# Selective attention with two key tiles per query tile, a bound checked on chip, and head-pair clusters between MLP subtiles

## The chip, the cores and the metric

The kernel runs on one core of a Trainium2 chip. The metric is device time in microseconds (us) of one execution; lower is better. The profile is one execution taken by the hardware profiler. Engines are named as there: PE is TensorE, PEld its weight loads, DVE is VectorE, ACT is ScalarE, POOL is GpSimd, SP is the queue that issues DMAs.

## The reference, cut to what matters

Causal attention over 8 batches, 8 heads, 576 tokens and 64 channels, with a penalty that grows with the summed positive part of `s` between key and query; then an MLP with exact GELU over the 4608 tokens.

```python
scores = scale * np.matmul(q, k.transpose(0, 1, 3, 2))
cum = np.cumsum(np.maximum(s, 0.0), axis=-1)
bias = -(cum[:, :, :, None] - cum[:, :, None, :])
scores = np.where(causal, -1000000000.0, scores + np.minimum(bias, 0.0))
attn = softmax(scores)            # with 1e-9 added to the sum
x = (attn @ v) as [4608, 512]
out = gelu_exact(x @ w_in) @ w_out    # 512 -> 2048 -> 512
```

`q`, `k` and `v` are normal draws times 0.1, `s` is a normal draw times 0.5, so `cum` rises by about 0.2 per token: a key 128 tokens back has a weight of about e^-25.

## The kernel before, in words

The penalty is a product: exp(cum of the key) goes into the values (`scale_v`, L158, with `wb`) and into the column of the denominator, and exp(-cum of the query) drops out in the quotient. So a head's attention is exp(scores), a mask on the diagonal tile, and two products with the same probabilities, one with the scaled values and one with `wb`.

Keys lie in five tiles of 128 (the last has 64). `UNITS` (L51) lists, per unit, the key tile, the first query, the number of queries and the place in PSUM; every key tile meets all later queries, 1600 columns per head. Two heads of a pair use the two halves of the PE array. `sc_item` (L232) is one unit of one pair: matmuls, one exp on ACT (L246), the mask on DVE (L254). `av_item` (L258) is one block of 256, 256 or 64 queries: numerator and denominator (L266), then Ln and Exp on ACT (L279, L280; the reciprocal) and the product into `xT` on DVE (L284).

The MLP works on nine chunks of 512 tokens. `l1_item` (L289): 8 matmuls of 512 columns and one GELU. `l2_item` (L305): a quarter of a 128-token subtile, 4 matmuls; after four quarters a copy to SBUF (L317) and a store.

Each engine runs its instructions in the order in which they are written (`manual_schedule`, L80). In chunk `c` (L373) the transposes of batch `c+1` (`tr_item`, L220, copies L228) lie between the L1 items; then `scale_v`, the table switch, the load and cast of batch `c+2`; then the 16 score items and 12 output items of batch `c+1` lie between 14 L2 quarters (`interleave`, L321). Chunks 7 and 8 have no attention beside them. Before the loop stand: the loads of batch 0, its casts and transposes, `scale_v(0)`, w_in, `load(1)`, the attention of batch 0 alone, `cast(1)`, w_out (L356 to L371). PSUM: `sc` (scores and L1) two buffers of two banks, `av` (outputs and transposes) two of one, `mlp` two of one.

Of the kernel before, what the change touches and what calls it, by code (L numbers as in the profile page):

```python
# [19 lines left out]
def kernel(  # L20
# [10 lines left out]
    nc = tc.nc  # L31
# [3 lines left out]
    MULT = mybir.AluOpType.mult  # L35

# [13 lines left out]

    UNITS = [  # L51
        [(0, 0, 512, 0)],
        [(1, 128, 448, 0), (0, 512, 64, 448)],
        [(2, 256, 320, 0), (3, 384, 192, 320)],
        [(4, 512, 64, 0)],
# [8 lines left out]
    LNC = [-28.0, 30.0, 60.0]  # L64
    ICH = [(0, 256), (256, 256), (512, 64)]
    PARTS, READY = [], []
    for c0, cn in ICH:
        parts = []
        for jt, i0, n, u, off in SEGS:
            lo, hi = max(i0, c0), min(i0 + n, c0 + cn)  # L70
            if lo < hi:
                parts.append((jt, lo - c0, hi - lo, off + lo - i0, u))
        parts.sort(key=lambda x: (-x[2], x[0]))
        PARTS.append(parts)
        READY.append(max(x[4] for x in parts))

    const = ctx.enter_context(tc.tile_pool(name="const", bufs=1))
    work = ctx.enter_context(tc.tile_pool(name="work", bufs=1))
    ps = ctx.enter_context(tc.tile_pool(name="ps", bufs=1, space=bass.MemoryType.PSUM))
    ctx.enter_context(tc.manual_schedule())  # L80
# [18 lines left out]
    nc.vector.tensor_copy(ident_bf, ident)  # L99
    lnb = const.tile([128, 3], fp32, name="lnb")  # L100
# [10 lines left out]
    qT = const.tile([128, NP, 640], bf16, name="qT")  # L111
    kT = const.tile([128, NP, 640], bf16, name="kT")
# [36 lines left out]

    def cast_pair(b, p):  # L150
        hs = slice(2 * p, 2 * p + 2)
        for i, n in enumerate(("q", "k")):
            t = raws[b, n]
            eng = nc.vector if i == 0 else nc.gpsimd
            eng.tensor_copy(qk_bf[:, i, 0 : ST - 1, hs], t[:, 0 : ST - 1, hs])
            eng.tensor_copy(qk_bf[:SL, i, ST - 1, hs], t[:SL, ST - 1, hs])
# [28 lines left out]

    def weights():
        s_pos = const.tile([64, S], fp32, name="s_pos")
        nc.vector.tensor_scalar_max(s_pos, s_sw, 0.0)
        sT = const.tile([128, ST, BH], fp32, name="sT")
        t_ps = ps.tile([128, ST, BH], fp32, tag="mlp", bufs=2, name="t_ps")  # L190
        for st in range(ST):
# [6 lines left out]
        c_ps = ps.tile([128, ST, BH], fp32, tag="mlp", bufs=2, name="c_ps")  # L198
        terms = [
            [(0, uptri_m1), (1, nones)],  # L200
            [(1, uptri_m1)],
            [(2, uptri)],
            [(2, ones), (3, uptri)],
            [(2, ones), (3, ones), (4, uptri)],
        ]
        for st in range(ST):
            n_st = 128 if st < ST - 1 else SL
            for i, (st2, m) in enumerate(terms[st]):
                n2 = 128 if st2 < ST - 1 else SL
                nc.tensor.matmul(  # L210
                    c_ps[:n_st, st, :], lhsT=m[:n2, :n_st], rhs=sT[:n2, st2, :],
                    start=(i == 0), stop=(i == len(terms[st]) - 1),
                )
# [5 lines left out]

    def tr_item(b, p, i):  # L220
        t_ps = ps.tile([128, 1024], bf16, tag="av", bufs=2, name="tr_ps")
        for st in range(ST):
            nc.tensor.transpose(  # L223
                t_ps[:, st * 128 : st * 128 + 128],
                qk_bf[:, i, st, 2 * p : 2 * p + 2, :].rearrange("p h d -> p (h d)"),
                ident_bf,
            )
        nc.vector.tensor_copy((qT, kT)[i][:, p, :S], t_ps[:, :S])  # L228
# [3 lines left out]
    def sc_item(b, p, u):  # L232
        if u == 0:
            P_of[b, p] = work.tile([128, 2, PW], bf16, tag="P", bufs=2, name="P")
        P = P_of[b, p]
        uw = UW[u]
        s_ps = ps.tile([128, 2, 512], fp32, tag="sc", bufs=2, name="sc_ps")
        for jt, i0, n, off in UNITS[u]:
            for e in range(2):
                nc.tensor.matmul(  # L240
                    s_ps[:, e, off : off + n],
                    lhsT=kT[e * 64 : e * 64 + 64, p, jt * 128 : jt * 128 + 128],
                    rhs=qT[e * 64 : e * 64 + 64, p, i0 : i0 + n],
                    start=True, stop=True,
                )
        nc.scalar.activation(  # L246
            P[:, :, UO[u] : UO[u] + uw], s_ps[:, :, :uw], func=AF.Exp, scale=scale
        )
        for jt, i0, n, off in UNITS[u]:
            if i0 != jt * 128:  # L250
                continue
            w = min(128, n)
            d = P[:, :, UO[u] + off : UO[u] + off + w]
            nc.vector.tensor_tensor(  # L254
                d, d, tri_bf[:, :w].unsqueeze(1).to_broadcast([128, 2, w]), op=MULT
            )

    def av_item(b, p, c):  # L258
        P = P_of[b, p]
        c0, cn = ICH[c]  # L260
        o_ps = ps.tile([128, 2, 256], fp32, tag="av", bufs=2, name="av")
        vb = vv[b % 2]
        for den in range(2):
            for n_part, (jt, lo, n, off, u) in enumerate(PARTS[c]):
                for e in range(2):
                    nc.tensor.matmul(  # L266
                        o_ps[e * 64 : e * 64 + 64, den, lo : lo + n],
                        lhsT=(
                            wb[:, jt, b * H + 2 * p + e : b * H + 2 * p + e + 1].to_broadcast([128, 64])
                            if den  # L270
                            else vb[:, jt, 2 * p + e, :]
                        ),
                        rhs=P[:, e, off : off + n],
                        start=(n_part == 0),
                        stop=n_part == len(PARTS[c]) - 1,
                        skip_group_check=True,
                    )
        ln = work.tile([128, 256], fp32, tag="ln", bufs=2, name="ln")
        nc.scalar.activation(ln[:, :cn], o_ps[:, 1, :cn], func=AF.Ln, scale=math.exp(-LNC[c]))  # L279
        nc.scalar.activation(  # L280
            ln[:, :cn], ln[:, :cn], func=AF.Exp, scale=-1.0, bias=lnb[:, c : c + 1]
        )
        t0 = b * S + c0
        nc.vector.tensor_tensor(xT[:, p, t0 : t0 + cn], o_ps[:, 0, :cn], ln[:, :cn], op=MULT)  # L284

# [3 lines left out]
    def l1_item(c, f2):  # L289
        if f2 == 0:  # L290
            gT_of[c] = work.tile([128, FT, NB], bf16, tag="gT", bufs=1, name="gT")
        h_ps = ps.tile([128, 2, NB], fp32, tag="sc", bufs=2, name="h_ps")
        for i in range(2):
            ft = f2 * 2 + i
            for ko in range(KO):
# [5 lines left out]
        nc.scalar.activation(gT_of[c][:, f2 * 2 : f2 * 2 + 2, :], h_ps, func=AF.Gelu)  # L301

    o_of = {}

    def l2_item(c, sub, part):  # L305
        if part == 0:
            o_of[c] = ps.tile([128, KO * 128], fp32, tag="mlp", bufs=2, name="o_ps")
        o_ps = o_of[c]
        gT = gT_of[c]
        for ft in range(part * 4, part * 4 + 4):  # L310
            nc.tensor.matmul(  # L311
                o_ps, lhsT=gT[:, ft, sub * 128 : (sub + 1) * 128], rhs=w_out_r[:, ft, :],
                start=(ft == 0), stop=(ft == FT - 1),
            )
        if part == 3:
            o_sb = work.tile([128, KO * 128], fp32, tag="osb", bufs=3, name="o_sb")
            nc.vector.tensor_copy(o_sb, o_ps)  # L317
            r0 = c * NB + sub * 128
            nc.sync.dma_start(out=out[r0 : r0 + 128, :], in_=o_sb)
# [18 lines left out]
    def attn_side(b, lag):  # L338

        items, due = [], []  # L340
        units = [(p, u) for p in range(NP) for u in range(NU)]
        for kk, (p, u) in enumerate(units):
            items.append(lambda p=p, u=u: sc_item(b, p, u))
            due += [(kk + lag, p, c) for c in range(len(ICH)) if READY[c] == u]
            while due and due[0][0] <= kk:
                _, p2, c2 = due.pop(0)
                items.append(lambda p=p2, c=c2: av_item(b, p, c))
        for _, p2, c2 in due:
            items.append(lambda p=p2, c=c2: av_item(b, p, c))
        return items  # L350

# [15 lines left out]
    for f in attn_side(0, 1):  # L367
        f()
    cast(1)
    for i in range(4):  # L370
        load_w(1, i)  # L371

    for c in range(NCH):  # L373
        nb = c + 1
        l1 = [lambda f2=f2: l1_item(c, f2) for f2 in range(FT // 2)]
        l2 = [lambda sub=sub, part=part: l2_item(c, sub, part) for sub in range(4) for part in range(4)]
        if nb < B:
            interleave(l1, tr_side(nb))
            scale_v(nb)
            exp_set()  # L380
            if nb + 1 < B:
                load(nb + 1)
                cast(nb + 1)
            interleave(l2[:14], attn_side(nb, 1), lead=1)
            for f in l2[14:]:
                f()
        else:
            for f in l1 + l2:
                f()
# [30 lines left out]
```

## Time and profile before

| | |
|---|---|
| median of 3 runs | 478.62 us (478.27 to 479.3) |
| the profiled execution | 474.67 us |
| its span, first to last instruction | 472.9 us |
| mean granted TensorE clock | 0.96 |
| busy | PE 391.3, ACT 263.7, DVE 177.1, POOL 44.2 us |

Read it by stages: a start until about 99 us, seven periods with attention beside the MLP, and two chunks of MLP alone. Busy time of PE counts each matmul from its start to its modelled end; what a matmul costs in a stream is the distance from one start to the next.

### The profile page before, as it was taken

To read this page: it belongs to the slowest core of one execution; us is meant where nothing else is said; L and a number is where in the kernel's file an instruction comes from. 1 tells how busy PE (TensorE), PEld (TensorE's weight loads), DVE (VectorE), ACT (ScalarE), POOL (GpSimd) and SP (SyncE) were. 2 spreads that over 40 slices of the span, in tenths; PEclk is the share of its full clock that TensorE was granted. 3 is DMA by queue.
4 is the path that set the end of the run, shared out by engine and by line. 5 is a ranking of instruction groups with operands and counts; after the bars stand their busy time and mean duration, and the time that the engine had idled before them with its cause. 6 is when DMAs were issued, how large, how long until landed. Compare 5 with 4: busy or idle time off the path is not lost.

```text
span 472.9 us, 8057 instructions
## 1 busy us (share of the span) xinstructions
PE 391.3 (83%) x3232; PEld 195.8 (41%) x3287; DVE 177.1 (37%) x425; ACT 263.7 (56%) x410; POOL 44.2 (9%) x49
## 2 busy tenths in 40 slices
PE   4310568579997999799979997999799989999996
PEld 4100334234453445344534453445344544444442
DVE  2314544264426442634263426342534244401101
ACT  1020575167846775677566756685658577751330
POOL 3100220040004000400040004000400000000000
PEclk9999967799999999999998999899989999999999
DMA  4448995960197019701870167118821000101101
GB/s 95 105 106 300 241 236 203 218 123 24 46 191 132 24 46 185 139 24 46 170 149 28 46 155 153 40 46 154 146 47 46 24 0 24 48 22 44 46 22 67
DMA packets 122757, 46.81 MB, mean 99 GB/s; under 512 B 113952, under 2 KB 113952, under 8 KB 122720
## 3 DMA queue, kind: packets, MB, share of 16 engines
q1 hardware_dynamic: 122720, 46.30, 42.3%
q8 instruction: 25, 0.41, 0.4%
q14 instruction: 12, 0.10, 0.1%
HBM read 36.85 MB, written 9.44 MB: 98 GB/s over the span
## 4 chain that ended last, share of the span: by engine, by line
PE 68%; DVE 10%; ACT 7%; SPq 7%; DMA 5%; issue 3%
PE h_ps L296 25%; PE o_ps L311 23%; PE av L266 13%; SPq L135 7%; ACT P L246 4%; PE sc_ps L240 4%; DVE vv_97 L163 3%; DVE vv_98 L163 3%; PE tr_ps L223 3%; DMA wf<-in_moe_w_in_dram 3%; DMA wf<-in_moe_w_out_dram 2%; DVE P L254 1%; ACT ln L279 1%; ACT ln L280 1%; DVE w_out_r L183 1%
## 5 line engine op out<-in xcount | busy, mean ns | idle before, releaser
L311 PE MATMUL o_ps<-w_out_r,gT 128*128 128x512 bf16 x538 | 140.3, 390 | 5.0 <-issue 4.4
L296 PE MATMUL h_ps<-xT,w_in_r 128*128 128x512 bf16 x559 | 135.2, 384 | 1.2 <-issue 0.3
L301 ACT ACTIVATE gT<-h_ps 128x1024 bf16<-128x1024 f32 x72 | 73.7, 1024 | 90.0 <-PE h_ps L296 90.0
L246 ACT ACTIVATE P<-sc_ps 128x1024 bf16<-128x1024 f32 (+1 forms) x128 | 102.8, 831 | 31.7 <-PE sc_ps L240 30.9
L296 PEld LDWEIGHTS <-w_in_r 128*128 128x128 bf16 x576 | 54.8, 99 | 58.0 <-issue 3.0
L311 PEld LDWEIGHTS <-gT 128*128 128x128 bf16 x576 | 48.4, 99 | 60.0 <-issue 13.2
L279 ACT ACTIVATE ln<-av 128x256 f32<-128x256 f32 (+1 forms) x96 | 31.4, 327 | 59.3 <-PE av L266 59.2
L254 DVE TENSOR_TENSOR P<-P,tri_bf 128x256 bf16<-128x256 bf16 (+1 forms) x160 | 42.5, 289 | 49.9 <-ACT P L246 49.8
L284 DVE TENSOR_TENSOR xT<-av,ln 128x256 bf16<-128x256 f32 (+1 forms) x96 | 34.3, 357 | 65.0 <-ACT ln L280 54.7
L266 PE MATMUL av<-P,vv_97 128*64 128x64 bf16 (+2 forms) x352 | 25.9, 256 | 34.2 <-DVE P L254 33.8
L240 PE MATMUL sc_ps<-qT,kT 64*128 64x64 bf16 (+4 forms) x384 | 43.6, 292 | 5.9 <-ACT P L246 5.9
L223 PE MATMUL tr_ps<-ident_bf,qk_bf 128*128 128x128 bf16 x320 | 30.6, 232 | 18.4 <-DVE qT L228 6.8
L280 ACT ACTIVATE ln<-ln,lnb 128x256 f32<-128x256 f32 (+1 forms) x96 | 43.6, 454 | 3.1
L317 DVE COPY o_sb<-o_ps 128x512 f32<-128x512 f32 x36 | 24.7, 686 | 53.0 <-PE o_ps L311 53.0
L266 PE MATMUL av<-P,wb 128*64 128x64 bf16 (+2 forms) x704 | 42.8, 240 | 0.0
L147 POOL CAST qk_bf<-raw_q 128x2048 bf16<-128x2048 f32 x7 | 13.3, 1896 | 272.9 <-DMA raw_k<-in_k_dram 126.3
L223 PEld LDWEIGHTS <-qk_bf 128*128 128x128 bf16 x320 | 24.2, 103 | 33.8 <-issue 7.6
L266 PEld LDWEIGHTS <-vv_97 128*64 128x64 bf16 x352 | 15.6, 120 | 49.0 <-issue 40.4
L228 DVE COPY kT<-tr_ps 128x576 bf16<-128x576 bf16 x32 | 14.6, 458 | 49.3 <-PE tr_ps L223 49.2
L240 PEld LDWEIGHTS <-kT 64*128 64x128 bf16 x384 | 15.0, 95 | 43.4 <-issue 37.5
L266 PE MATMUL av<-P,vv_98 128*64 128x64 bf16 (+2 forms) x352 | 23.5, 238 | 8.3 <-DVE P L254 7.8
L228 DVE COPY qT<-tr_ps 128x576 bf16<-128x576 bf16 x32 | 14.6, 458 | 41.7 <-PE tr_ps L223 41.7
(51 smaller groups left out, 159.7 us busy)
## 6 DMA issues: line engine op xcount, KB each, us to landing
out_dram<-o_sb SPq DMA_DIRECT2D x36, 256.0 KB, 2.0
raw_q<-in_q_dram SPq DMA_DIRECT2D x28, 256.0 KB, 5.0
raw_k<-in_k_dram SPq DMA_DIRECT2D x28, 256.0 KB, 5.4
raw_v<-in_v_dram SPq DMA_DIRECT2D x28, 256.0 KB, 4.5
wf<-in_moe_w_in_dram SPq DMA_DIRECT2D x4, 1024.0 KB, 5.3
wf<-in_moe_w_out_dram SPq DMA_DIRECT2D x4, 1024.0 KB, 7.7
raw_q<-in_q_dram SPq DMA_DIRECT2D x16, 64.0 KB, 2.2
raw_k<-in_k_dram SPq DMA_DIRECT2D x16, 64.0 KB, 2.2
```

The source lines that it names most:

```text
L135: nc.sync.dma_start(out=t[:n_st, st, h0 : h0 + hn, :], in_=bass.AP(tensor=src2.tensor, offset=src2.offset + (b * H + h0) * S * D + st * 12 ...
L223: nc.tensor.transpose(t_ps[:, st * 128 : st * 128 + 128], qk_bf[:, i, st, 2 * p : 2 * p + 2, :].rearrange("p h d -> p (h d)"), ident_bf,)
L240: nc.tensor.matmul(s_ps[:, e, off : off + n], lhsT=kT[e * 64 : e * 64 + 64, p, jt * 128 : jt * 128 + 128], rhs=qT[e * 64 : e * 64 + 64, p, ...
L246: nc.scalar.activation(P[:, :, UO[u] : UO[u] + uw], s_ps[:, :, :uw], func=AF.Exp, scale=scale)
L254: nc.vector.tensor_tensor(d, d, tri_bf[:, :w].unsqueeze(1).to_broadcast([128, 2, w]), op=MULT)
L266: nc.tensor.matmul(o_ps[e * 64 : e * 64 + 64, den, lo : lo + n], lhsT=(wb[:, jt, b * H + 2 * p + e : b * H + 2 * p + e + 1].to_broadcast([ ...
L279: nc.scalar.activation(ln[:, :cn], o_ps[:, 1, :cn], func=AF.Ln, scale=math.exp(-LNC[c]))
L280: nc.scalar.activation(ln[:, :cn], ln[:, :cn], func=AF.Exp, scale=-1.0, bias=lnb[:, c : c + 1])
L284: nc.vector.tensor_tensor(xT[:, p, t0 : t0 + cn], o_ps[:, 0, :cn], ln[:, :cn], op=MULT)
L296: nc.tensor.matmul(h_ps[:, i, :], lhsT=w_in_r[:, ko, ft * 128 : (ft + 1) * 128], rhs=xT[:, ko, c * NB : (c + 1) * NB], start=(ko == 0), st ...
L301: nc.scalar.activation(gT_of[c][:, f2 * 2 : f2 * 2 + 2, :], h_ps, func=AF.Gelu)
L311: nc.tensor.matmul(o_ps, lhsT=gT[:, ft, sub * 128 : (sub + 1) * 128], rhs=w_out_r[:, ft, :], start=(ft == 0), stop=(ft == FT - 1),)
```

## The change

Each query block meets two key tiles (256 columns per key tile, 192 and 64 at the end): 1024 columns per head, in two units. What is left out is bounded: `absmax` takes the largest |q| and |k| on DVE, `square_v` sums v squared on POOL, `cert_decay` and `cert_end` compare sums of the penalties and weights with limits, and one value `bad` decides at the end whether a general path, which computes everything anew with all keys, runs. With the inputs of the reference every comparison holds, worked out from them on paper (the largest: 67.5 against 78, 69.4 against 78, 0.256 against 0.375, 0.26 against 1), so the general path is skipped.

The order changes too. All scores of a pair and all outputs of the pair before it form one cluster, and whole L2 subtiles of 16 matmuls stand between clusters. L1 begins with two items without their last quarter. The last transposes stand behind L1. `load` and `cast` of batch `c+2` move behind the first L2 subtile and behind `square_v`. `av` gets three PSUM buffers, `mlp` one.

```diff
     UNITS = [
-        [(0, 0, 512, 0)],
-        [(1, 128, 448, 0), (0, 512, 64, 448)],
-        [(2, 256, 320, 0), (3, 384, 192, 320)],
-        [(4, 512, 64, 0)],
+        [(0, 0, 256, 0), (1, 128, 256, 256)],
+        [(2, 256, 256, 0), (3, 384, 192, 256), (4, 512, 64, 448)],
     ]
...
+    def absmax(b, p):
+        nc.vector.tensor_reduce(
+            amx[:, b * NP + p], qkT[:, :, p, :S], axis=AX, op=ALU.max, apply_absolute_value=True
+        )
+    def square_v(b):
+        t = raws[b, "v"]
+        for st in range(ST):
+            n_st = 128 if st < ST - 1 else SL
+            sq = work.tile([128, H, D], fp32, tag="sq", bufs=2, name="sq")
+            nc.gpsimd.tensor_tensor(sq[:n_st], t[:n_st, st], t[:n_st, st], op=MULT)
+            nc.gpsimd.tensor_tensor(sumv[:n_st], sumv[:n_st], sq[:n_st], op=ALU.add)
...
+    def cert_decay():
+        t_ps = ps.tile([1, ST + 1, BH], fp32, tag="av", bufs=3, name="ct_ps")
+        for st in range(ST):
+            n_st = 128 if st < ST - 1 else SL
+            nc.tensor.matmul(t_ps[:, st, :], lhsT=ones[:n_st, 0:1], rhs=sT[:n_st, st, :], start=True, stop=True)
...
+        nc.vector.tensor_copy(T, t_ps)
+        nc.vector.tensor_copy(W, w_ps)
...
+    def cert_end():
+        g = const.tile([128, 3], fp32, name="cg")
+        for i in range(2):
+            nc.vector.tensor_reduce(g[:, i : i + 1], amx[:, :, i], axis=AX, op=ALU.max)
+        nc.vector.tensor_reduce(
+            g[:, 2:3], sumv.rearrange("p h d -> p (h d)"), axis=AX, op=ALU.max
+        )
+        g_ps = ps.tile([3, 128], fp32, tag="av", bufs=3, name="cg_ps")
+        nc.tensor.transpose(g_ps, g, ident)
+        g3 = const.tile([3, 1], fp32, name="cg3")
+        nc.vector.tensor_reduce(g3, g_ps, axis=AX, op=ALU.max)
+        h_ps = ps.tile([1, 3], fp32, tag="av", bufs=3, name="ch_ps")
+        nc.tensor.transpose(h_ps, g3, ident[:3, :3])
...
+    def sc_item(b, p):
+        P_of[b, p] = P = work.tile([128, 2, PW], bf16, tag="P", bufs=2, name="P")
+        for u in range(NU):
+            s_ps = ps.tile([128, 2, 512], fp32, tag="sc", bufs=2, name="sc_ps")
...
+            nc.scalar.activation(
+                P[:, :, UO[u] : UO[u] + UW[u]], s_ps[:, :, : UW[u]], func=AF.Exp, scale=scale
+            )
+            d = P[:, :, UO[u] : UO[u] + 512].rearrange("p e (g c) -> p e g c", c=256)[:, :, :, 0:128]
+            nc.vector.tensor_tensor(
+                d, d, tri_bf.unsqueeze(1).unsqueeze(1).to_broadcast([128, 2, 2, 128]), op=MULT
+            )
+            if u == 1:
...
+    def av_item(b, p):
...
+        for c, (c0, cn) in enumerate(ICH):
+            o_ps = ps.tile([128, 2, 256], fp32, tag="av", bufs=3, name="av")
...
+            todo.append(o_ps)
+        for c, (c0, cn) in enumerate(ICH):
...
-    def l2_item(c, sub, part):
-        if part == 0:
-            o_of[c] = ps.tile([128, KO * 128], fp32, tag="mlp", bufs=2, name="o_ps")
+    def l2_item(c, sub):
         gT = gT_of[c]
-        for ft in range(part * 4, part * 4 + 4):
+        o_ps = ps.tile([128, KO * 128], fp32, tag="mlp", bufs=1, name="o_ps")
+        for ft in range(FT):
...
-    for f in attn_side(0, 1):
-        f()
+    for p in range(NP):
+        sc_item(0, p)
+        if p > 0:
+            av_item(0, p - 1)
+    av_item(0, NP - 1)
+    for p in range(NP):
+        absmax(0, p)
+    square_v(0)
     cast(1)
     for i in range(4):
         load_w(1, i)
+    cert_decay()
     for c in range(NCH):
         nb = c + 1
+        l1_item(c, 0, 0, KO - 1)
+        l1_item(c, 1, 0, KO - 1)
+        l1_item(c, 0, KO - 1)
+        l1_item(c, 1, KO - 1)
+        l1 = [lambda f2=f2: l1_item(c, f2) for f2 in range(2, FT // 2)]
         if nb < B:
-            interleave(l1, tr_side(nb))
+            tr = tr_side(nb)
+            interleave(l1, tr[:4])
+            for f in tr[4:]:
+                f()
             scale_v(nb)
             exp_set()
-            if nb + 1 < B:
-                load(nb + 1)
-                cast(nb + 1)
-            interleave(l2[:14], attn_side(nb, 1), lead=1)
-            for f in l2[14:]:
+            for p in range(NP):
+                sc_item(nb, p)
+                if p > 0:
+                    av_item(nb, p - 1)
+                l2_item(c, p)
+                absmax(nb, p)
+                if p == 0:
+                    square_v(nb)
+                    if nb + 1 < B:
+                        load(nb + 1)
+                        cast(nb + 1)
+            av_item(nb, NP - 1)
+        else:
+            for f in l1:
                 f()
-        else:
-            for f in l1 + l2:
-                f()
+            for sub in range(4):
+                l2_item(c, sub)
+            if c == B - 1:
+                cert_end()
+    fast.close()
+    rv = nc.values_load(bad[0:1, 0:1], min_val=0, max_val=1)
+    with tc.If(rv > 0):
...
```

## Rows read from the trace of the kernel before

**Rows 1.** The page: the chain that ended last, shares of the span by engine.
```profile
PE 68%; DVE 10%; ACT 7%; SPq 7%; DMA 5%; issue 3%
```

**Rows 2.** Windows by stage; columns in the first line.
```profile
core 0: us, PE busy (x) PEld busy (x) DVE busy (x) ACT busy (x) POOL busy (x), PEclk, DMA share, GB/s
130.45:178.30 47.85, 43.97 (x385) 21.75 (x392) 20.21 (x50) 31.93 (x51) 5.30 (x4) 0.96 0.49 97
...
369.56:414.36 44.80, 42.75 (x385) 21.37 (x392) 18.18 (x50) 31.86 (x51) 0.00 (x0) 1.00 0.07 25
...
152.00:153.50 1.50, 1.50 (x10) 0.69 (x10) 0.53 (x3) 0.60 (x2) 0.00 (x0) 0.50 0.81 116
153.50:155.40 1.90, 1.90 (x15) 0.84 (x15) 0.65 (x2) 0.57 (x2) 0.00 (x0) 0.56 0.02 4
```

**Rows 3.** Timeline of PE in L1: start, length, engine, line, count.
```profile
131.53 0.44 PE L223 MATMUL tr_ps<-ident_bf,qk_bf 128*128 128x128 bf16 x5
...
131.81 1.89 PE L296 MATMUL h_ps<-xT,w_in_r 128*128 128x512 bf16 x8
...
133.53 0.44 PE L223 MATMUL tr_ps<-ident_bf,qk_bf 128*128 128x128 bf16 x5
```

**Rows 4.** Timeline of PE among scores, outputs and L2 quarters.
```profile
107.05 0.57 PE L266 MATMUL av<-P,vv_98 128*64 128x256 bf16 x8
...
107.94 1.04 PE L311 MATMUL o_ps<-w_out_r,gT 128*128 128x512 bf16 x4
108.91 0.39 PE L240 MATMUL sc_ps<-qT,kT 64*128 64x512 bf16 x2
...
110.64 0.61 PE L240 MATMUL sc_ps<-qT,kT 64*128 64x448 bf16 x8
111.18 1.04 PE L311 MATMUL o_ps<-w_out_r,gT 128*128 128x512 bf16 x4
...
122.17 0.35 PE L266 MATMUL av<-P,vv_98 128*64 128x64 bf16 x10
...
122.61 1.04 PE L311 MATMUL o_ps<-w_out_r,gT 128*128 128x512 bf16 x4
```

**Rows 5.** Timeline where L1 gives way to attention; idle time and releaser in brackets.
```profile
144.07 1.90 POOL L147 CAST qk_bf<-raw_q 128x2048 bf16<-128x2048 f32 x1 [41.27 <-DMA raw_k<-in_k_dram]
...
146.42 5.30 DVE L163 TENSOR_TENSOR vv_97<-raw_v,wb 128x512 bf16<-128x512 f32 x5
...
151.98 0.53 PE L266 MATMUL av<-P,vv_97 128*64 128x256 bf16 x4 [2.40 <-DVE P L254]
```

**Rows 6.** The same DVE instructions in the last period with attention.
```profile
385.53 3.08 DVE L163 TENSOR_TENSOR vv_98<-raw_v,wb 128x512 bf16<-128x512 f32 x5
```

**Rows 7.** Groups by line: count | busy us, mean ns | idle before, releaser.
```profile
L246 ACT ACTIVATE P<-sc_ps 128x1024 bf16<-128x1024 f32 x96 | 94.3, 1019 | 26.0 <-PE sc_ps L240 25.2
...
L279 ACT ACTIVATE ln<-av 128x256 f32<-128x256 f32 (+1 forms) x96 | 31.4, 327 | 59.3 <-PE av L266 59.2
...
L280 ACT ACTIVATE ln<-ln,lnb 128x256 f32<-128x256 f32 (+1 forms) x96 | 43.6, 454 | 3.1
...
L317 DVE COPY o_sb<-o_ps 128x512 f32<-128x512 f32 x36 | 24.7, 686 | 53.0 <-PE o_ps L311 53.0
...
L155 POOL CAST qk_bf<-raw_k 128x512 bf16<-128x512 f32 x4 | 2.5, 615 | 18.0 <-DMA raw_k<-in_k_dram 18.0
```

**Rows 8.** Timeline at the end of the start: last w_out cast, PE, first score.
```profile
86.05 1.23 DVE L183 CAST w_out_r<-wf 128x2048 bf16<-128x2048 f32 x1 [4.02 <-DMA wf<-in_moe_w_out_dram]
...
87.70 0.69 PE L223 MATMUL tr_ps<-ident_bf,qk_bf 128*128 128x128 bf16 x5 [6.81 <-DVE qT L228]
...
99.37 0.39 PE L240 MATMUL sc_ps<-qT,kT 64*128 64x512 bf16 x2
```

**Rows 9.** The end: last copy (timeline); SP's waits: us, times, longest.
```profile
469.18 0.69 DVE L317 COPY o_sb<-o_ps 128x512 f32<-128x512 f32 x1 [2.76 <-PE o_ps L311]
...
SPq L415 <- PEq L415: 0.6, 2, 0.4
```

## Prediction before the run

> **What bounds the kernel now.** I read the page first, then the windows by stage, then PE's timeline inside a period. The chain of waits runs through PE for 68% of the span [rows 1], so the sum is one of PE's time, and other engines count where PE waits for them. Three kinds of stage follow the start [rows 2]: six periods of L1, transposes, attention and L2 (47.85 us in the one shown), a last such period without a load (44.80), and from 414.4 two chunks of MLP alone. A bare chunk is 128 matmuls of 512 columns. Eight of them take 133.53 - 131.81 = 1.72 us [rows 3], so a chunk takes 27.5, and attention costs a period about 20 us of PE. That is what the change cuts.
>
> Inside the period PE is dense but for one hole: the first output matmuls wait 2.40 us for the mask on DVE, which stands behind `scale_v` [rows 5], and after it the granted clock is 0.50, the lower of the two levels, 1.2 GHz, for 1.5 us and on average 0.56 for the next 1.9 [rows 2]: that costs 0.75 + 0.84 = 1.6 us more. In the last period the same five products take 3.08 us instead of 5.30 [rows 5, 6], POOL has no cast beside them, the clock stays at 1.00, and the period is 3.05 us shorter. So a POOL cast beside DVE's two-input products costs 3 us a period.
>
> **L1 with transposes.** A group of five transposes costs 131.81 - 131.53 = 0.28 us. The head (two items of six matmuls, then two of two) makes 14 matmuls before the first GELU can start, at 3.0 us; the GELU has the shape of the exp, which takes 1.02 [rows 7]; the third item needs its PSUM buffer, so it starts at 4.3 instead of 3.45. This is a new stall of 0.85 in all nine chunks. It buys the cover for the last output block: its Ln, Exp and product may end 2.6 us later than L1 begins. Then 6 x 1.72 + 3 x 0.28 = 11.15, and five transpose groups at the end, 1.7 us with three buffers. L1 ends at 17.15. The last GELU hides behind these transposes.
>
> **A cluster.** Scores: two units of 512 columns take 111.18 - 110.64 = 0.54 [rows 4]; before, four units. Outputs: the 256-query block took 107.94 - 107.05 = 0.89 for 1792 columns on a half of the array, 0.50 ns each, the last block 122.61 - 122.17 = 0.44 for 640, 0.69 ns each. After, 28 matmuls of 2048 columns in all: 1.02 by the one, 1.41 by the other; I take 1.2, since the wide blocks hold most columns. An L2 quarter takes 108.91 - 107.94 = 0.97, that is 0.86 and about 0.11 for the change of shape; a whole subtile 3.45 + 0.11 = 3.56. A pair costs 0.54 + 1.2 + 3.56 = 5.3.
>
> Do the others keep up? ACT per pair: two exps 2.04, and (31.4 + 43.6) / 32 = 2.34 for Ln and Exp [rows 7], 4.4 of 5.3. DVE: masks and products of 1728 elements 2.1 (by `scale_v`'s 0.62 for 512 [rows 6]), the copy 0.69 [rows 7], and the new `absmax` over 1152 elements. No such reduce is in the trace; by `scale_v`'s 3.08 for five times 512 [rows 6] it takes 1.4, by the copy's 0.69 for 512 [rows 7] 1.55, below that if bf16 runs faster; I take 1.4. Sum 4.2 of 5.3. The order also fits: output of pair p-1 comes a whole subtile after its exp, so a mask has 4 us to arrive. The first outputs come at 17.15 + 0.54 + 3.56 + 0.54 = 21.8, `scale_v` (from 17.8, 3.08) and two masks end at about 21.9. The hole of 2.40 us is covered by the subtile, as long as POOL is quiet.
>
> Attention is then 4 x 5.3 + 0.3 = 21.5, the period 38.65; with 0.3 for a mask that meets a cast I take **39.0**, against 47.85. Bounds: outputs 1.02 to 1.41 give 38.0 to 39.9.
>
> **The load and POOL.** `load` and `cast` go behind the first L2 subtile's store, 22 us into the period instead of at its start. The casts started 13.6 us into the period shown [rows 5], when the data had landed; now at about 35, with some 5 us of work, ending 1.5 us into the next L1. The first transposes come at 7.8, so 6 us of cover stay; each us beyond that would be PE's. On SP the stores of three subtiles queue behind 15 load issues; nobody waits, as the three output buffers last a period. SP's issue of v now also waits for `square_v` of the batch before, done 20 us earlier.
>
> `square_v` adds ten POOL instructions of 512 elements with two inputs per batch. The nearest row is the cast of 512 elements, one input, 0.615 [rows 7]; two inputs should lie between 0.6 and 1.25, and I take 1.2. The Trainium skill (GPSIMD Engine Reference, section on elementwise cycle accounting) gives 4497 ns for 2048 elements of such an add, an estimate of 1.12 for 512; by that the sum stays as it is. They run after the casts and after v has landed (half of what q and k took, 6.8 us later, at 42), so from 3 to 15 us into L1, where DVE only copies from PSUM. `scale_v` follows at 17.8. So the contention of before should vanish here, and by the same margin of 2.8 us it could come back (rivals).
>
> **The two bare chunks.** With one `mlp` buffer and nothing between subtiles, PE's next matmul waits for the copy, 0.69 [rows 7], and two hand-overs: 0.7 to 1.2, I take 0.95, three times in each chunk; behind it the rest of L2 is queued on PE and the GELUs of the next chunk on ACT. A chunk is 27.5 + 0.85 + 2.85 = 31.2. `cert_end` puts two transposes in front of L1 of the last chunk: PE waits for the copy (0.95), three reduces (about 0.9) and a further small reduce between them, 3.0 us with latencies (2 to 4.5), and then runs at the lower clock as after the 2.40 us hole, 1.6 more. Sum 31.2 + 3.0 + 1.6 + 31.2 = **67.0**, against 55.0.
>
> **The start.** Before, PE stood until 87.70 for DVE copies behind the last w_out cast, and the first score of batch 1 came 11.7 us later, at 99.37 [rows 8]. After, that cast moves: four `absmax` (5.6) are put in front of it, `square_v(0)` meets `scale_v(0)` and the w_in casts (0 to 5, I take 3), the attention of batch 0 is shorter (a pair by 0.54 for scores and, at 0.50 to 0.69 ns for 1152 columns, 0.6 to 0.8 for outputs, twice that at the lower clock; four pairs 5 to 10, I take 7), and `load(2)` no longer takes bandwidth (1). About 0.6 later: PE goes on at 88.3. `cert_decay` adds some 20 tiny DVE instructions behind it, about 3 us, covered by L1. With three `av` buffers PE has done five L1 items by then instead of three, so three are left: 5.2 + 0.85 for transposes, 1.7 for the last groups, 1.6 at the lower clock: scores start at 97.7 (92 to 102). I credit almost nothing here.
>
> **The tail.** From the last copy's start at 469.18 [rows 9] to the end of the span are 3.7 us, 3.9 with the hand-over before it; they stay. The register load, the branch and their barriers have no row; the nearest are SP's waits for other engines at the end, 0.6 together [rows 9], and that last chain itself, 3.7, done up to three times, 11. I take 5, nearer the low end, as only one value is read. The Trainium skill (Runtime: NRT & Kernel Launch, instruction fetch mechanics) says that a taken branch out of the fetched pages stalls for a fetch; no row shows one, and by that rule the 5 would be nearer 7.
>
> **The sum.** 97.7 + 21.5 (batch 1) + 6 x 39.0 + 67.0 + 3.9 + 5 = 429.1 of span, against 472.9. Around the span lie 474.67 - 472.9 = 1.8: 430.9. The median of the runs shown is 478.62, 0.83% over the profiled execution, so **434.5 us**.
>
> **The rivals.**
> (a) POOL meets `scale_v` and stops the next period: the squares run to 42 + 10X, that is 3 + 10X into L1. At X = 1.2 they end before 17.8. From X = 1.6 on they hold `scale_v` and the first masks, and PE waits 10X - 17 us in every period, plus 1.6 at the lower clock. Rows 5 and 6 show the mechanism; against it stands the 0.615 of rows 7. X = 1.6 to 2.1 gives 439 to 475. The page SBUF — State Buffer of the Trainium skill (Who interferes with whom) states that a GpSimd instruction and a two-input DVE instruction exclude each other for a whole instruction; 5.30 against 3.08 agrees.
> (b) Slower: the same place, X above 2.2. Then 7 x (10X - 15.4) is more than the 44 gained: 2.5 gives 502. It needs an instruction 3.6 times as long as the cast of as many elements.
> (c) DVE becomes the bound of the clusters: if `absmax` takes over 2.5 us, each further us costs 28. At 3.0, 449.
> (d) The bound fails and the general path runs: several milliseconds. The inputs speak against it.
> (e) Better: outputs at 0.50 ns (5 us), the start without contention (5) and a tail of 1 (4) give 420.
>
> **How the numbers follow.** Forecast (425 to 444) 0.55, (a) 0.14, (b) 0.06, (c) 0.07, (d) 0.01, (e) 0.13; the remaining 0.04 is a mixture that ends near the old time. The range takes in (e)'s end, (c) and most of (a): 419 to 460. Changes within 0.2% can't be told from none in this kernel. Slower by more than that: (b), (d) and half the mixture, 0.08; same 0.02; faster 0.90.
>
> **What would show it.** A window between two first L1 matmuls of 39 us with the clock at 1.00; `scale_v` at 3.1 us; squares at 1.2 each, ended before it; no idle time of PE before `av`; PE idle 0.95 before `o_ps` in the last chunks, released by DVE's copy; a gap of 3 us before the last L1. It would be wrong if PE waits in `av` for DVE while POOL is busy, if ACT has no idle time between exps, or if the pair takes over 5.6 with PE dense.

## The result and the profile after

The changed kernel takes 417.73 us (median of 4 runs, 416.19 to 418.4) against 478.44 for the kernel before in 4 runs: a ratio of 0.873, interval 0.870 to 0.877. The forecast was 434.5; the time lies 1.3 us below the low end of its range. The profiled execution took 417.87 us with a span of 416.0.

The chain of waits still runs through PE, now for three quarters of the span (before: [rows 1]):

```profile
PE 75%; SPq 8%; DMA 7%; DVE 4%; ACT 3%; issue 2%; ACTq 0%; DVEq 0%
```

Windows by stage, with the columns of [rows 2]: two of the six periods, then the two bare chunks.

```profile
116.24:153.95 37.71, 37.03 (x321) 20.03 (x322) 21.90 (x46) 26.60 (x43) 15.50 (x14) 1.00 0.59 120
153.95:191.67 37.72, 37.04 (x322) 20.02 (x322) 21.55 (x46) 26.61 (x43) 16.88 (x15) 1.00 0.61 125
...
342.52:372.00 29.48, 26.45 (x122) 11.65 (x121) 3.98 (x7) 11.01 (x14) 0.00 (x0) 1.00 0.10 36
372.00:416.00 44.00, 32.42 (x139) 13.69 (x137) 9.08 (x31) 8.08 (x8) 0.00 (x0) 0.91 0.09 32
```

A period fell from 47.85 to 37.71 us, and in it PE is busy for 37.03 us at full clock: 0.68 us is left, the stall in the head of L1. Of these windows the clock dips only in the last, behind the check's last comparison.

The timeline of POOL and DVE where L1 gives way to attention, the place of [rows 5]: first and last square, `scale_v`, the first masks.

```profile
156.50 1.03 POOL L173 TENSOR_TENSOR sq<-raw_v 128x512 f32<-128x512 f32 x1
157.61 1.27 POOL L174 TENSOR_TENSOR sumv<-sumv,sq 128x512 f32<-128x512 f32 x1
...
166.97 1.26 POOL L174 TENSOR_TENSOR sumv<-sumv,sq 64x512 f32<-64x512 f32 x1
...
171.70 3.08 DVE L189 TENSOR_TENSOR vv_101<-raw_v,wb 128x512 bf16<-128x512 f32 x5
174.70 0.75 DVE L357 TENSOR_TENSOR P<-P,tri_bf 128x512 bf16<-128x512 bf16 x2
```

The squares end 3.5 us ahead of `scale_v`, which takes the 3.08 us that it took before without a cast beside it [rows 6]. PE's waits say the same from the other side (us in total, times, longest):

```profile
PE av L375 <- DVE P L357: 23.7, 1, 23.7
PE tr_ps L332 <- DVE cT L268: 6.2, 1, 6.2
PE h_ps L413 <- ACT gT L419: 6.2, 9, 0.7
...
PE o_ps L425 <- DVE o_sb L430: 4.7, 6, 0.8
...
PE cg_ps L302 <- DVE cg L298: 1.6, 1, 1.6
```

PE waits for a mask once in the whole execution, in the start. The hole of 2.40 us in each period is gone.

The outputs of a pair on PE, with the next matmul behind them, and the last copy:

```profile
341.44 0.35 PE L375 MATMUL av<-P,vv_101 128*64 128x256 bf16 x4
341.63 0.33 PE L375 MATMUL av<-P,wb 128*64 128x256 bf16 x4
341.79 0.39 PE L375 MATMUL av<-P,vv_101 128*64 128x256 bf16 x6
342.01 0.39 PE L375 MATMUL av<-P,wb 128*64 128x256 bf16 x6
342.23 0.23 PE L375 MATMUL av<-P,vv_101 128*64 128x64 bf16 x4
342.29 0.23 PE L375 MATMUL av<-P,wb 128*64 128x64 bf16 x4
342.46 2.76 PE L413 MATMUL h_ps<-xT,w_in_r 128*128 128x512 bf16 x12
...
409.48 0.69 DVE L430 COPY o_sb<-o_ps 128x512 f32<-128x512 f32 x1 [3.70 <-PE o_ps L425]
```

The 28 output matmuls take 342.46 - 341.44 = 1.02 us. The last copy starts 6.5 us ahead of the end of the span; before it was 3.7 [rows 9].

### The profile page after: what moved, and what is told of

It is laid out like the page before. It is cut to its first block, busy times and chain, and to the rows that moved or that the text cites. A ratio compares the mean times of both kernels' runs of the same rounds, so it can differ in the third digit from the quotient of the medians.

```text
span 416.0 us, 7091 instructions
## 1 busy us (share of the span) xinstructions
PE 348.8 (84%) x2745; PEld 187.6 (45%) x2745; DVE 207.1 (50%) x441; ACT 221.3 (53%) x346; POOL 140.3 (34%) x130
## 4 chain that ended last, share of the span: by engine, by line
PE 75%; SPq 8%; DMA 7%; DVE 4%; ACT 3%; issue 2%; ACTq 0%; DVEq 0%
PE o_ps L425 31%; PE h_ps L413 28%; SPq L146 8%; PE av L375 8%; PE tr_ps L332 4%; PE sc_ps L347 4%; DMA wf<-in_moe_w_in_dram 3%; DMA wf<-in_moe_w_out_dram 3%; ACT gT L419 2%; DVE o_sb L430 1%; DVE w_out_r L209 1%; ACT P L353 1%; DVE w_in_r L203 1%; ACT ln L391 0%; ACT ln L392 0%
## 5 line engine op out<-in xcount | busy, mean ns | idle before, releaser
L425 PE MATMUL o_ps<-w_out_r,gT 128*128 128x512 bf16 x576 | 130.5, 379 | 4.7 <-DVE o_sb L430 4.7
L353 ACT ACTIVATE P<-sc_ps 128x1024 bf16<-128x1024 f32 x64 | 61.9, 1021 | 40.9 <-PE sc_ps L347 40.9
L337 DVE COPY qkT<-tr_ps 128x576 bf16<-128x576 bf16 x64 | 26.6, 453 | 85.2 <-PE tr_ps L332 85.0
L174 POOL TENSOR_TENSOR sumv<-sumv,sq 128x512 f32<-128x512 f32 (+1 forms) x40 | 52.1, 1302 | 3.1
L173 POOL TENSOR_TENSOR sq<-raw_v 128x512 f32<-128x512 f32 (+1 forms) x40 | 47.0, 1174 | 9.3 <-DMA raw_v<-in_v_dram 9.3
L163 DVE TENSOR_REDUCE amx<-qkT 128x2 f32<-128x1152 bf16 x32 | 42.7, 1341 | 0.0
L396 DVE TENSOR_TENSOR xT<-av,ln 128x256 bf16<-128x256 f32 (+1 forms) x96 | 33.7, 357 | 17.6 <-ACT ln L392 15.5
L375 PE MATMUL av<-P,vv_100 128*64 128x128 bf16 (+2 forms) x224 | 17.2, 248 | 27.1 <-DVE P L357 23.7
L375 PE MATMUL av<-P,wb 128*64 128x128 bf16 (+2 forms) x448 | 28.8, 237 | 0.0
L357 DVE TENSOR_TENSOR P<-P,tri_bf 128x512 bf16<-128x512 bf16 x64 | 27.4, 451 | 2.0 <-ACT P L353 1.7
L158 POOL CAST qk_bf<-raw_k 128x2048 bf16<-128x2048 f32 x7 | 13.3, 1894 | 27.8 <-DMA raw_k<-in_k_dram 15.6
```

The source lines that it names most:

```text
L163: nc.vector.tensor_reduce(amx[:, b * NP + p], qkT[:, :, p, :S], axis=AX, op=ALU.max, apply_absolute_value=True)
L173: nc.gpsimd.tensor_tensor(sq[:n_st], t[:n_st, st], t[:n_st, st], op=MULT)
L174: nc.gpsimd.tensor_tensor(sumv[:n_st], sumv[:n_st], sq[:n_st], op=ALU.add)
L353: nc.scalar.activation(P[:, :, UO[u] : UO[u] + UW[u]], s_ps[:, :, : UW[u]], func=AF.Exp, scale=scale)
L375: nc.tensor.matmul(o_ps[e * 64 : e * 64 + 64, den, lo : lo + n], lhsT=(wb[:, jt, b * H + 2 * p + e : b * H + 2 * p + e + 1].to_broadcast([ ...
L425: nc.tensor.matmul(o_ps, lhsT=gT[:, ft, sub * 128 : (sub + 1) * 128], rhs=w_out_r[:, ft, :], start=(ft == 0), stop=(ft == FT - 1),)
```

## The experiments

Each of the nine was timed beside the kernel before on the same chip; its medians there were 476.6 to 478.3 us. A difference between the medians of two experiments, or between one of them and 417.73, is therefore good to about 2 us; where less than that matters, the traces are compared. In every expectation, a "theory" is the prediction's sum with the terms that the trace after shows.

### Tiles alone, order alone

`e1_tiles_only`: the kernel before with one edit.

```diff
     UNITS = [
-        [(0, 0, 512, 0)],
-        [(1, 128, 448, 0), (0, 512, 64, 448)],
-        [(2, 256, 320, 0), (3, 384, 192, 320)],
-        [(4, 512, 64, 0)],
+        [(0, 0, 256, 0), (1, 128, 256, 256)],
+        [(2, 256, 256, 0), (3, 384, 192, 256), (4, 512, 64, 448)],
     ]
```

> The kernel before with the two-tile UNITS alone (1024 columns per head in two units), its order, its buffers and no bound computed: it leaves out the check and the general path. Theory (PE time of the dropped columns pays what it costs, the hole stays): a pair saves 0.54 us of scores and 0.6 to 0.8 of outputs, so a period goes from 47.85 to about 43 with the wait of about 2.4 us of the outputs for the mask, the low clock behind it and products of 5.3 us in scale_v still there; seven periods 34, the attention of batch 0 alone another 5 to 7: about 438 us (430 to 445). Rival (the order carries most of the gain, the columns little since PE then waits for ACT and DVE): 455 or more.

Measured: 445.47 us, ratio 0.936 (0.932 to 0.939): 31 us less, half of the whole gain, half a microsecond above the theory's range and 7.5 above its 438. The period is 44.06 instead of 47.85. The timeline shows what stays:

```profile
139.84 5.29 DVE L161 TENSOR_TENSOR vv<-raw_v,wb 128x512 bf16<-128x512 f32 x5
...
145.38 0.53 PE L264 MATMUL av<-P,vv 128*64 128x256 bf16 x4 [3.37 <-DVE P L252]
```

`scale_v` still takes 5.29, and PE waits 3.37 for the mask instead of 2.40: the scores in front of it got shorter, DVE's work did not. A part of what the tiles save goes into the wait.

`e2_order_only`: the changed kernel with the old `UNITS`, and masks by key tile as before.

```diff
     UNITS = [
-        [(0, 0, 256, 0), (1, 128, 256, 256)],
-        [(2, 256, 256, 0), (3, 384, 192, 256), (4, 512, 64, 448)],
+        [(0, 0, 512, 0)],
+        [(1, 128, 448, 0), (0, 512, 64, 448)],
+        [(2, 256, 320, 0), (3, 384, 192, 320)],
+        [(4, 512, 64, 0)],
     ]
```

> The changed kernel with the old UNITS (1600 columns per head, four units, a mask per key tile): the new order, buffers and check without the dropped columns. Theory (the clusters live from having two score units for two PSUM buffers): the third and fourth unit of a pair wait for exps of about 1.02 us each, a pair costs about 8 us instead of 5.1, a period about 49 to 51: 485 to 515 us, slower than before. Rival (the order is worth something by itself, since it closes the hole of 2.4 us and keeps the clock): 440 to 465.

Measured: 496.4 us, 1.042 (1.038 to 1.046), slower than before. PE's waits name the cause:

```profile
PE sc_ps L349 <- ACT P L355: 48.2, 65, 1.4
```

65 waits of a score unit for the exp that frees its PSUM buffer, 48.2 us; in the changed kernel there are two, 1.0 us, both in the start. The 496.4 hold the check too, which the next experiment prices at 16 us, so the order by itself gains nothing: its periods take 48.2 us (from the head's wait at 184.61 to that at 232.82) against 47.85 before. What it wins elsewhere, the hole and the low clock behind it among them, it loses at the two buffers: in that period these waits add up to 6.05 us. On top of the tiles it is worth 6.35 us a period, 44.06 - 37.71.

### What the check costs

`e3_no_check`: the calls of `absmax`, `square_v`, `cert_decay`, `cert_end` and everything from `values_load` on removed.

> The changed kernel without the bound check: no absmax, no squares, no cert_decay, no cert_end, no branch and no general path; that part is left out. Theory (in the periods the check is hidden on DVE and POOL; it costs only where PE or the end waits for it): tail -2.8, the gap before the last chunk -2.35 and its low clock -1.7, the start -2 to -3 (5.1 us of absmax in front of DMA-paced w_out casts): 408 us (405 to 411), periods still 37.7. Rival (the check also costs in the periods, by shared ports or DVE's turn): periods of 36.5 or less, 400 us or less.

Measured: 401.6 us, 0.842 (0.838 to 0.846), below the theory's range: the check costs 16 us by the medians and 15.0 by the profiled spans (416.0 and 401.0), not 10. The periods are not where it lies:

```profile
112.47:150.18 37.71, 37.03 (x320) 20.02 (x320) 17.03 (x41) 26.59 (x43) 4.89 (x4) 1.00 0.54 115
```

37.71 us with and without the check, though DVE falls from 21.9 to 17.0 busy and POOL from 15.5 to 4.9. The rival falls. The tail is 3.7 again (last copy at 397.31, span 401.0), so the register load and the branch cost 2.8. The rest is in the start: the first L1 matmul behind the attention of batch 1 comes at 108.16 instead of 116.17, 8.0 earlier where 2 to 3 were expected.

`e8_decay_early` looks for these 8 us.

```diff
     weights()
+    cert_decay()
     for p in range(NP):
         cast_pair(0, p)
...
         load_w(1, i)
-    cert_decay()
```

> The changed kernel with cert_decay moved from behind the w_out casts to right behind the computation of the weights, where PE and DVE wait for q and k. Theory (the check's cost in the start is mostly cert_decay: 2.8 us of fp32 matmuls on PE in front of the first L1, and 4.2 us of small DVE instructions between the last w_out cast and the copies of the transposes): 7 us less, about 411 us (409.5 to 413). Rival (the start is paced by the w_out loads, and the part of cert_decay is hidden behind them; the cost lies in absmax and the squares): 416 to 418.

Measured: 410.03 us, 0.859 (0.854 to 0.863): moving one call gives 7.7 us. The lines of after that explain it, with the last w_out cast and the DVE instructions behind it:

```profile
66.50 1.31 PE L260 MATMUL ct_ps<-sT,ones 128*1 128x64 f32 x10 [0.23 <-DVE xT L396]
...
84.13 1.23 DVE L209 CAST w_out_r<-wf 128x2048 bf16<-128x2048 f32 x1 [1.87 <-DMA wf<-in_moe_w_out_dram]
85.27 0.54 DVE L268 COPY cT<-ct_ps 1x384 f32<-1x384 f32 x1
...
85.86 0.69 PE L332 MATMUL tr_ps<-ident_bf,qk_bf 128*128 128x128 bf16 x5 [6.22 <-DVE cT L268]
```

`cert_decay` puts its matmuls in front of L1 (from 66.50 to 69.29) and then holds two of the three `av` buffers until DVE copies them out, and that copy stands behind w_out casts that wait for their loads. PE's second group of transposes needs a buffer, waits 6.2 us for the copy, and three items of L1 stand behind it on PE. In e8 PE does all eight items of L1 before it waits, 1.88 us at the fourth group of transposes, and the first score comes at 87.60 instead of 95.69, 8.1 earlier. The edit moves the matmuls, the two buffers and the DVE instructions at once, so it prices the call and not the buffers alone. An estimate from these two traces: with the buffers free and the DVE instructions left in place, PE would wait at the fourth group for copies that begin at 89.44 instead of e8's 84.68, and the first score would come near 92.4; by that some 4.8 of the 8.1 us are DVE's queue and 3.3 the buffers. No run separates the two. What is left of the check's cost in the start is 410.03 - 401.6 less the tail's 2.8 and the 4.0 of the last comparison, 1.6 us, for `absmax` and the squares together; by the profiled spans (408.3 and 401.0) it is 0.5.

`e5_absmax_twice`: one more `absmax(nb, p)` behind the one in the loop.

> The changed kernel with absmax done twice per pair for batches 1 to 7: 1.34 us more of DVE in each of 28 pairs, about 5.4 us of DVE per pair of 5.12 us. Theory (DVE has about 1 us of room per pair and the masks have a subtile of lead, so only the excess shows): 418 to 430 us. Rival (DVE already sets the pace of the clusters): 28 times 1.34, about 455 us. The other rival (DVE has room of its own beyond what the sum of its durations says): 417 to 419.

Measured: 426.27 us, 0.891 (0.887 to 0.895): +8.5 us, where every instruction on the path would have given 37.5. Its windows for two neighbouring periods:

```profile
163.53:204.60 41.07, 37.36 (x320) 20.25 (x320) 29.00 (x49) 26.58 (x43) 19.47 (x18) 1.00 0.62 128
204.60:242.53 37.93, 37.20 (x321) 20.02 (x321) 25.79 (x49) 26.60 (x43) 11.86 (x11) 1.00 0.54 99
```

In the second, 5.4 us more of DVE cost 0.2 us. In the first a POOL cast of q or k meets the small mask (1.91 us instead of 0.22, twice in that period); DVE, with 29.0 us of work in that stretch, does not make it up, and PE waits up to 1.86 us for the next product. So DVE is not the bound, but the room that it has is what absorbs such meetings, and the doubled reduce uses it up. (The first of these periods loses 3.4 us; the attention of batch 1 has the same two meetings and loses about as much, and chunk 0 lost about 1.4, as the last w_out cast came that much later.)

`e4_squares_twice`: the two POOL instructions of `square_v` in a loop of two for batches 2 to 7.

> The changed kernel with each instruction of square_v done twice for batches 2 to 7: about 23.4 us of POOL per batch instead of 11.7, so that the squares end about 26 us into L1, past the start of scale_v at 17.8. Theory (rival (a) of the prediction: POOL beside DVE's two-input products holds them and the masks, and the first outputs wait): scale_v above 5 us, PE waits in front of the first outputs, some 8 us in each of six periods: about 466 us (450 to 475). Rival (POOL is off the path whatever it does): 416 to 420.

Measured: 457.45 us, 0.957 (0.954 to 0.959), 39.7 above the changed kernel: rival (a) of the prediction, brought about. Its timeline around the last square and the first outputs, then windows of one period and of the five products:

```profile
178.82 7.69 DVE L190 TENSOR_TENSOR vv<-raw_v,wb 128x512 bf16<-128x512 f32 x5
...
184.37 1.59 POOL L175 TENSOR_TENSOR sumv<-sumv,sq 64x512 f32<-64x512 f32 x1
...
186.89 0.53 PE L376 MATMUL av<-P,vv 128*64 128x256 bf16 x4 [3.94 <-DVE P L358]
```

```profile
165.31:209.54 44.23, 39.60 (x320) 21.35 (x320) 27.12 (x45) 26.75 (x43) 29.09 (x24) 0.92 0.51 106
178.82:186.51 7.69, 4.13 (x28) 1.95 (x27) 7.69 (x7) 4.09 (x5) 6.90 (x5) 0.92 0.00 0
```

The five products take 7.69 us instead of 3.08, PE waits 3.94, the granted clock of the period falls from 1.00 to 0.92, and the period grows by 6.5 us, 39 in six. The law of the prediction gave 8.0: the wait came out 2.5 us shorter than 10X - 17 with X = 2.34, and what is lost beside the wait, 2.6 us, larger than its 1.6. In the stretch of the products the DMA share is 0.00, so it is POOL that they meet there. The Trainium skill (SBUF — State Buffer, Who interferes with whom) states that a two-input DVE instruction and a GpSimd instruction that reads SBUF shut each other out; these 7.69 us agree.

### The hole of the kernel before

`e6_before_casts_early`: the kernel before, with the POOL cast moved away from `scale_v`.

```diff
-    qk_bf = const.tile([128, 2, ST, H, D], bf16, name="qk_bf")
+    qk_bfs = [const.tile([128, 2, ST, H, D], bf16, name=f"qk_bf{i}") for i in range(2)]
...
+                def then_load(f11=f11, b2=nb + 2):
+                    f11()
+                    load(b2, which="qk")
+                    cast(b2)
+                l2[11] = then_load
```

> The kernel before, its columns and order kept, with two buffers for the cast q and k; q and k of batch b+2 are loaded behind the twelfth L2 quarter of the period before and cast there on POOL, so that no POOL cast stands beside scale_v of the next period. Theory (POOL's cast beside DVE's two-input products makes scale_v 5.3 us instead of 3.1, the outputs wait 2.4 us for it, and the clock falls behind that wait): 2.5 to 3 us less in each of the five or six periods that have such a cast: 460 to 465 us. Rival (the products are slow for another reason, or the next wait takes the place of this one): 474 to 479.

Measured: 456.75 us, 0.959 (0.954 to 0.964), 3.3 below the theory's range. From its timeline, and a window of one period:

```profile
142.79 3.08 DVE L168 TENSOR_TENSOR vv<-raw_v,wb 128x512 bf16<-128x512 f32 x5
...
146.13 0.30 PE L271 MATMUL av<-P,vv 128*64 128x256 bf16 x2 [0.18 <-DVE P L259]
```

```profile
127.90:172.71 44.81, 43.54 (x393) 21.37 (x392) 18.21 (x49) 31.89 (x50) 4.96 (x4) 1.00 0.53 104
```

The period is 44.81, that of the last period before [rows 2]: 3.04 us less, six times 18 us. The edit takes more than the cast away from `scale_v`: the loads of q and k move too. Windows of the five products, first one of the kernel before, then that of batch 1 in e6:

```profile
146.42:151.72 5.30, 2.50 (x15) 0.93 (x15) 5.30 (x7) 4.51 (x5) 2.96 (x3) 1.00 0.94 178
97.98:101.06 3.08, 2.50 (x16) 0.82 (x15) 3.08 (x7) 3.05 (x4) 0.00 (x0) 1.00 0.66 136
```

In the kernel before, the products run beside POOL and beside loads, with a DMA share of 0.94. For batch 1 of e6 loads still run beside them, with a share of 0.66, POOL is idle, and they take 3.08; in e4 POOL works without any load beside it, and they take 7.69. So it is the cast and not the load: the reading of rows 2, 5 and 6 is shown. It also means that a third of the change's gain can be had in the kernel before, with all columns and no check.

### Versions that are faster than both

`e7_mended`: three edits of the changed kernel.

```diff
-        o_ps = ps.tile([128, KO * 128], fp32, tag="mlp", bufs=1, name="o_ps")
+        alone = c + 1 >= B and sub % 2
+        o_ps = ps.tile(
+            [128, KO * 128], fp32, tag="av" if alone else "mlp", bufs=3 if alone else 1, name="o_ps"
+        )
...
         l1_item(c, 1, KO - 1)
+        tr = tr_side(nb) if nb < B else []
+        for f in tr[:2]:
+            f()
...
+            parts = cert_end() if c == B - 1 else iter(())
             for f in l1:
                 f()
+                next(parts, None)
```

> The changed kernel with three edits that go at its remaining waits of PE: in the two bare chunks the subtile's PSUM tile alternates between two pools, the last comparison is cut into steps that stand between the L1 items of chunk 7, and the first two groups of transposes stand in the gap of L1's head. Theory: the six waits of 0.95 us before o_ps go (-5.7), the gap of 2.35 and the low clock of 1.7 go (-4.0), 0.56 us of transposes hide in a stall of 0.7 in each of seven periods (-3.9): 404 us (401 to 408). Rival (the clock gate takes it back: gapless PE runs at a lower granted clock, or DVE's steps delay the copies of the transposes): 412 to 418.

Measured: 408.63 us, 0.857 (0.853 to 0.861). That is 0.6 above the theory's range. Each edit did what it was to do, and one did harm besides. From its timeline, a window of one period, and PE's waits:

```profile
358.50 13.98 PE L432 MATMUL o_ps<-w_out_r,gT 128*128 128x512 bf16 x64
```

```profile
120.60:157.77 37.17, 37.05 (x326) 20.06 (x322) 21.45 (x46) 26.61 (x43) 16.57 (x15) 1.00 0.67 127
```

```profile
PE tr_ps L336 <- DVE cT L268: 10.3, 1, 10.3
```

The 64 matmuls of a bare chunk's L2 run as one block, the period is 0.54 shorter, the last comparison leaves no gap. But in chunk 0 the transposes now stand in the head, and meet the wait for `cT` with six items of L1 behind them: 10.3 us instead of 6.2, and the first score at 100.11 instead of 95.69. Without these 4.4 us it would be 404.2, an estimate that lies at the theory's value.

`e9_better` mends the start too: v of batch 0 in 5 loads instead of 20, `cert_decay` as in e8, and

```diff
-    for i in range(4):
-        load_w(0, i)
-    load(1)
     for p in range(NP):
         sc_item(0, p)
         if p > 0:
             av_item(0, p - 1)
+        load_w(0, p)
+        absmax(0, p)
+    load(1)
     av_item(0, NP - 1)
...
+                wo = [lambda i=i: load_w(1, i) for i in range(4)]
+                interleave(l1, [wo[0], tr[0], tr[1], wo[1], tr[2], tr[3]])
+                for f in tr[4:6] + wo[2:3] + tr[6:8] + wo[3:4]:
+                    f()
```

> The mended kernel with a new start: v of batch 0 in 5 loads instead of 20, cert_decay behind the weights, the w_in casts of DVE between the pairs of batch 0's attention instead of in front of it, the w_out casts between the copies of chunk 0's transposes, and chunk 0 without transposes in its head. Theory (PE's wait of 24 us for the first mask of batch 0 is DVE's queue: w_in casts paced by loads stand in front of the masks; SP issues 20 loads of v at 0.6 us each in front of w_in): the first L1 begins some 14 us earlier, the loads of w_out then hold it by a few: 388 to 397 us. Rival (the start is bound by the bytes that must land, so an order of the casts changes little): 403 to 406, which is the mended kernel without its wait of 4.4 us in chunk 0.

Measured: 390.7 us, 0.818 (0.816 to 0.821), 6.5% below the changed kernel. From the timeline of after, then of e9:

```profile
53.93 0.53 PE L375 MATMUL av<-P,vv_100 128*64 128x256 bf16 x4 [23.68 <-DVE P L357]
69.29 4.06 PE L413 MATMUL h_ps<-xT,w_in_r 128*128 128x512 bf16 x16
```

```profile
37.22 0.53 PE L380 MATMUL av<-P,vv 128*64 128x256 bf16 x4 [5.05 <-DVE P L362]
...
53.96 5.45 PE L418 MATMUL h_ps<-xT,w_in_r 128*128 128x512 bf16 x16
...
78.82 1.04 PE L352 MATMUL sc_ps<-qkT 64*128 64x256 bf16 x10
```

PE's longest wait, 23.7 us for the first mask, was DVE's queue: the mask stood behind w_in casts that wait for loads. It is 5.05 now, shorter waits for products of DVE (4.02, 1.11 and 2.91) follow it, and L1 begins 15 us earlier. The edits of the start were not tried one by one.

## Why the prediction was wrong

In the periods the mechanism was right and the sizes were wrong; in the start a mechanism was wrong and the value came out near by luck. The terms that were mis-sized are the outputs of a pair, the margins, the tail and the step from the profile to the median. The sum, term by term, against the trace after:

| term | predicted | measured | difference |
|---|---|---|---|
| first score of batch 1 | 97.7 | 95.69 | -2.0 |
| attention of batch 1 (to 116.17) | 21.5 | 20.48 | -1.0 |
| six periods (to 342.46) | 6 x 39.0 | 6 x 37.715 | -7.7 |
| bare chunks, to the last copy's start | 67.2 | 67.02 | -0.2 |
| last copy to the end of the span | 8.7 | 6.5 | -2.2 |
| profiled execution to median | +3.6 | -0.1 | -3.7 |

Together -16.8.

- **Outputs of a pair.** "I take 1.2" between 1.02 and 1.41; it is 1.02, the price per column of the wide block of [rows 4], narrow block and all. Four pairs in seven batches: 5.0 us. This is the largest single miss.
- **Margins without a row.** The 0.3 for the entry of the clusters and 0.3 for a mask that meets a cast: 4.2 us in seven batches, and PE waits for neither. A mask did meet a cast (0.82 us instead of 0.42, at 150.19), but a whole subtile lay in front of its use.
- **The rest of a period** was as worked out: scores 0.55, a subtile 3.56, `scale_v` 3.08, squares 1.03 and 1.26 alone (taken as 1.2), `absmax` 1.34 (taken as 1.4), squares done 3.5 us before `scale_v`. The stall of the L1 head is 0.68, not 0.85.
- **The start** is near its value for a wrong reason. The sum had 8.6 us for `absmax` and the squares, and nothing for `cert_decay`, "covered by L1"; e3 and e8 show at most 1.6 for the first and 7.7 for the second. The step that failed here is the cover. With three `av` buffers for the transposes the order of the kernel lets all eight items of L1 pass before PE waits, as e8 does, and none would be left as a cover. The five items done and three left, which the prediction counts, came about only because `cert_decay` held two of the three buffers, which it did not count. The two errors met, so 97.7 against 95.69 is luck.
- **The bare chunks** hold: waits before `o_ps` of 0.78 idle, 0.95 with the hand-over, six times; a gap of 2.35 us instead of 3.0; 1.7 at the lower clock instead of 1.6.
- **The tail.** 5 us for load and branch, 2.8 by after and by e3. The Trainium skill's rule on branches (Runtime: NRT & Kernel Launch, instruction fetch mechanics), which in the prediction would have made it nearer 7, had no effect that a row here shows.
- **The 0.83%.** The profiled execution before lay at the low edge of its kernel's own scatter (473.6 to 479.3 over all runs here); it was no ratio between profile and median, and should have been a term of the range only.

The low end of 419 was that of rival (e) alone, whose outputs came in whole and its tail by half. The choices above were independent of one another, and all four came out too dear: 1.2 of 1.02 to 1.41, which is the middle, margins of 0.6, which have one sign only, 5 of 0.6 to 11, +0.83%. A range that took the low ends of these four together (5.0, 4.2, 4.4 and 3.6 us) would have reached 417.3. Rivals (a) and (c) did not happen. e4 brings (a) about, with squares of twice the time. e5 puts 2.68 us of reduces into a pair, beyond the 2.5 of (c), and DVE is still not the bound: a period without a meeting of mask and cast lost 0.2 us.

## What to carry to other kernels

Cutting work off PE pays only as far as the engines in front of it follow: the tiles alone gave half, the order alone nothing, and together both. When small work is moved under the cover of a larger stage, count the buffers that it holds and the queue that stands before its release, not only its instructions. Margins that no row asks for add up as surely as costs: they all have the same sign, and that is a bias, not caution.

## What the runs showed of the hardware

- Squares on POOL slow DVE's casts too, which have one input: two w_out casts took 1.89 and 1.84 us beside squares in the changed kernel, the two after the squares 1.23, and all four 1.23 in e3, which has no squares.
- Of POOL's two-input instructions over 512 elements, the square (the same tile twice) takes 1.03 us alone and the sum of two tiles 1.26; beside DVE's products in e9 they took 1.49 and 1.59.
- SP spends about 0.6 us on each small load (twenty of v in 12.12 in e3). With five loads of v instead of twenty, e9 issued the first w_in load at 28.56 instead of 36.06 in the changed kernel.
- A reduce over 1152 bf16 elements takes 1.34 us; the estimates from float32 instructions were 1.4 and 1.55, so the narrow type gave it little.
